# A state-space scan mixed with an FFT convolution on one core: the convolution rebuilt

## The chip, the cores and the metric

The kernel runs on one core of a Trainium2 chip. Its engines work beside each other, each through its own list of instructions in order: TensorE (PE) multiplies matrices into PSUM, with weight loads (PEld) as instructions of their own; VectorE (DVE) and ScalarE (ACT) compute on SBUF and PSUM; GpSimd (POOL) computes on SBUF and issues DMAs that add what they carry to what is there; SyncE (SP) issues plain and transposing DMAs. Sixteen DMA engines carry all transfers. Semaphores order the engines. The metric is the time of one execution on the device, in microseconds; lower is better.

## The reference

Two sequence models read the same x (2048 steps of 1024 channels, bf16) and a gate per step mixes them:

```python
g = sigmoid((x * gate_w).sum(-1, keepdims=True))
# a: a diagonal complex state space model with 1024 states
h = Lam_bar * h + Bu[:, t]            # for every t; Bu = x @ B_bar.T, complex
a = 2.0 * einsum(hseq, Cmat).real + x * Dskip
# b: a shift convolution of 4 taps, then a long one of 2048 taps, per channel
k_shift = sum over t of k_pad[:, t:t+S] * shift_k[:, ks-1-t]
kv = k_shift * v
y = irfft(rfft(pad(kv)) * rfft(pad(ssm_k)))[:S] + kv * ssm_D
b = x * y                             # q is x
out = g * a + (1 - g) * b             # g * a: also the term with Dskip
```

## The kernel before

**The long convolution (branch b)** is done by channels: 8 chunks `c` of 128 channels. A sequence of 2048 steps is cut into 4 blocks of 512. Each block is turned into 512 frequencies (four tiles `fi` of 128) by matmuls with tables of cosines and sines (CF, SF; NCF and NSF are negated halves), blocks are multiplied with one another, and a second pair of tables (CI, SI) brings the sums back. The tables use that a block can be split into an even and an odd part about its middle, which halves the matmuls: so every block is first folded, upper half plus and minus the mirrored lower half.

For chunk `c` the steps are:

- `load` (160): kT and vT, the channels of k and v with time along the row, and kn, the long kernel with time on the partitions, all by transposing DMAs of 512 KB.
- `taps` (430, through `tap_sums` 421): the 4 taps of the shift convolution as 16 matmuls of 512 columns, diagonal weights `dg` (built by `dgs` 252 on ACT), kT moving. ACT brings the sums to `ks`.
- `times_v` (454): DVE multiplies ks with vT, the lower halves of the blocks in reversed order (`lo`), the upper ones in place.
- `fold_V` (462): 16 matmuls of 256 columns turn the product to time on the partitions, and with the signs in PM at once into even and odd parts; 2 evacuations by ACT give `eov`.
- `fold_K` (406): the same for kn with an identity and a mirrored identity (`refl`) as weights: 8 matmuls of 512 columns, and two with one row that put ssm_D into the first tap; 2 evacuations give `eok`.
- `fwd_K` (475) and `fwd_V` (497): the spectra Kh and Vh, for half of the frequencies at a time (`hf`), so two tiles `fi` a call; an evacuation by ACT for each `fi`.
- `products` (511): for each half `hf` the complex products of all pairs of blocks whose sum of indices stays below 4: 8 products into scratch `t` and 11 sums into G, all on DVE.
- `inverse` (546): 32 matmuls of 512 columns from G, PSUM called psz, two evacuations to `cv`, and 4 DMAs that write the result to a scratch `cv_scr` in DRAM, laid out as [time, channel].

`turn_table` (373) makes one of 8 pairs of tables of turning angles for the scan (TC, TS, and TCi, TSi, scaled by the input gains); it is cut by `yield` into steps that are spread over the loop. `state_params` (312) does the small arithmetic of the states, on DVE.

**The state space model (branch a)** is done by blocks `tb` of 512 steps and groups `g` of 256 states. `Bu` (595) projects x: 32 matmuls of 512 columns and two evacuations to U. `scan` (606) on DVE turns U by the tables, runs 4 scans along time, and turns back, to `hb`. `Cy` (699) multiplies 128 steps of hb with CT (the transposed C) in 32 matmuls. `loads` (658) reads the rows of branch b from cv_scr (pbb) and of x; `scale_b` scales by 1 - g and adds the Dskip row with an adding DMA; `finish` (705) multiplies by x, adds both branches and stores.

**The order** is written out by hand. `put` (95) makes every instruction of an engine (DMA queues of SP and POOL too) follow the one issued before it, so the program's order is that of each engine. In the loop over chunks (764 to 819), for chunk `c` with n = c + 1 and nn = c + 2, PE does fold_K(n), half of the inverse of c - 1, half of fwd_K(n), fold_V(n), the other half of the inverse, half of fwd_V(n), taps(nn), and the other halves of fwd_K(n) and fwd_V(n), while DVE multiplies the spectra of chunk c. Buffers let PE run ahead: 6 half spectra (kvh), 4 half G, 4 + 3 scratch tiles (u4, w4), 3 double PSUM buffers and 2 single ones.

Lines 829 to 862 finish the convolution and interleave the last two turn tables with Bu of the first three groups. From 864 on come the tiles of the second part, the remaining Bu, and the loop (892) of one Cy, one Bu and one scan per turn; 8 of the 16 CT loads come before 862, 8 after it. From 911 on the last 512 steps: all groups but the last for 4 row tiles, then the last one in two halves.

Of the kernel before, what the change touches and what calls it, by code (L numbers as in the profile page):

```python
# [20 lines left out]
def kernel(  # L21
# [42 lines left out]
    NFI = 4  # L64

# [5 lines left out]
    cv_scr = dram.tile([S, D], BF16, name="cv_scr")  # L71
# [3 lines left out]
    wk = pool("wk", 3)  # L75
    wu = pool("wu", 4)
    psum = pool("psum", 3, space=bass.MemoryType.PSUM)
    psum1 = pool("psum1", 1, space=bass.MemoryType.PSUM)

    def w4(shape, dt, name):  # L80
        return wk.tile(shape, dt, name=name, tag="w4")
# [6 lines left out]

    def ps1(tag):
        return psum1.tile([128, 512], F32, name=tag, tag=tag)  # L90
# [25 lines left out]

    def copy(o, a):
        put("dve", V.tensor_copy, o, a)
# [21 lines left out]
    kv_pool = h3pool(h3, "kvh", 6)  # L140
    g_pool = h3pool(h3, "gh", 4)
    cv_pool = h3pool(h3, "cv", 2)
    tab_pool = h3pool(h3, "tab", 1)
    ld = h3pool(h3r, "ld", 3, side="right")
    ks_pool = h3pool(h3r, "ks", 2, side="right")
    eo_pool = h3pool(h3r, "eo", 2, side="right")
# [5 lines left out]
    prow = rows_[64:96, 0:128]  # L152

    nc.scalar.dma_start(out=skr, in_=B_shift_k.rearrange("(j p) k -> j p k", p=128))
    for i, ap in enumerate((A_Lambda_re, A_Lambda_im, A_log_dt, gate_w)):
        nc.scalar.dma_start(out=prow[i * 8:(i + 1) * 8, :], in_=ap.rearrange("(j p) -> j p", p=128))
# [4 lines left out]
    def load(which, c):  # L161
        cc = slice(c * 128, (c + 1) * 128)
        if which == "kn":

            t = ld.tile([128, NT, 128], BF16, name="kn", tag="ld")
            load_t(t, B_ssm_k[cc, :])
        else:
            t = ld.tile([128, S], BF16, name=which, tag="ld")
            load_t(t, (kf if which == "kT" else vf)[:, cc])
        lds[which, c] = t  # L170

    load("kT", 0)
    load("vT", 0)
# [5 lines left out]
    def load_BT(g):  # L179
        for c, src in enumerate((A_B_re, A_B_im)):  # L180
            load_t(BT[g][:, c], src[g * 256:(g + 1) * 256, :])

    def load_xT(tb, home=None):
        xT = (home or xt_pool).tile([128, ND, TB], BF16, name="xT")
        load_t(xT, xf[tb * TB:(tb + 1) * TB, :])
        xTs[tb] = xT
# [22 lines left out]
    def sincos(rq, n, sin_out, cos_out, sin_scale):  # L209

        fa = u4([128, n], F32, "fa")
        act(fa, rq, func=ACT.Abs)
        act(sin_out, rq, func=ACT.Sin, scale=sin_scale)
        act(cos_out, fa, func=ACT.Sin, bias=pih, scale=-TWO_PI)
# [7 lines left out]

    zeros = w4([128, 512], BF16, "zeros")
    put("dve", V.memset, zeros, 0.0)
    pih = consts.tile([128, 1], F32, name="pih")
    put("dve", V.memset, pih, math.pi / 2.0)
# [8 lines left out]
    colm_i = iota_i32([128, 2], [[256, 2]], 1, 2, "colm")  # L235
    fr_i = iota_i32([128, 2, 256], [[2, 2], [4, 256]], 1, 0, "fr_")
# [6 lines left out]
    pcol = consts.tile([128, 4 + KS, ND], F32, name="pcol")  # L243
    gwb = consts.tile([128, ND], BF16, name="gwb")
    psp = ps1("p1")[:, 0:32 + ND * KS]
    raise_clock(3)
    for k in range(KS):
        mm(psp[:, 32 + ND * k:32 + ND * (k + 1)], skr[:, :, k], ident[32:32 + ND, 32:32 + ND], True, True)
    raise_clock(6)
    copy(pcol[:, 4:], psp[:, 32:].rearrange("p (i j) -> p i j", j=ND))  # L250

    def dgs(c, on_dve=False):
        dg = ks_pool.tile([128, KS, 128], BF16, name="dg", bufs=1)
        for k in range(KS):
            if on_dve:
                ts(dg[:, k], ident, pcol[:, 4 + k, c:c + 1], None, ALU.mult)
            else:
                act(dg[:, k], ident, func=ACT.Identity, scale=pcol[:, 4 + k, c:c + 1])
        return dg

    dg0 = dgs(0, True)
    colm = consts.tile([128, 2], F32, name="colm")
    ts(colm, colm_i, 1.0 / 4096.0, None, ALU.mult)
    fr_ = u4([128, 512], F32, "fr_")
    copy(fr_, flat(fr_i))
    hf = u4([128, 2, 512], F32, "h")
    for mt in range(2):
        ts(hf[:, mt], fr_, colm[:, mt:mt + 1], None, ALU.mult)
    rqf = reduced(flat(hf), 1024)
    put("dve", V.scalar_tensor_tensor, out=flat(hf), in0=rqf, scalar=-1.0, in1=rqf, op0=ALU.mult, op1=ALU.max)  # L270
    PM = consts.tile([128, 2, 2, 128], BF16, name="PM")
    for a in range(2):
        for b in range(2):
            ts(PM[:, a, b], ident, -1.0 if a and b else 1.0, None, ALU.mult)

# [9 lines left out]
    def inverse_angles(h2):  # L285
        hi = (w4 if h2 else u4)([128, 2, 512], F32, "h")
        for k in range(2):
            fi = 2 * h2 + k
            ts(hi[:, k], trow[0], inv["col"][:, fi:fi + 1], inv["at0"][:, fi:fi + 1], ALU.mult, ALU.add)
        rq = (u4 if h2 else w4)([128, 1024], F32, "rq")  # L290
        ts(rq, flat(hi), MAGIC, -MAGIC, ALU.add, ALU.add)
        tt(flat(hi), flat(hi), rq, ALU.subtract)
        return flat(hi)

    def inverse_table(h2, rq):
        sincos(rq, 1024, flat(SI[:, 2 * h2:2 * h2 + 2]), flat(CI[:, 2 * h2:2 * h2 + 2]), -TWO_PI)


    Lre, Lim, logdt = pcol[:, 0], pcol[:, 1], pcol[:, 2]
# [4 lines left out]
    TC = rot_pool.tile([128, NP, TB], BF16, name="TC")  # L304
    TS = rot_pool.tile([128, NP, TB], BF16, name="TS")
    TCi = rot_pool.tile([128, NP, TB], BF16, name="TCi")
    TSi = rot_pool.tile([128, NP, TB], BF16, name="TSi")
# [4 lines left out]
    def state_params():  # L312

        mm(psp[:, 0:32], prow, ident[64:96, 64:96], True, True)
        copy(pcol[:, 0:4], psp[:, 0:32].rearrange("p (i j) -> p i j", j=ND))
        copy(gwb, psp[:, 24:32])
        yield
# [12 lines left out]
        for x, name in ((thn, "th"), (thU, "thU")):  # L330
# [4 lines left out]
            frs.append(fr)  # L335
        sc = []
# [11 lines left out]
        tt(rc, rv, cth, ALU.mult)  # L348
        rs = small("rs")
        tt(rs, rv, sth, ALU.mult)  # L350
        nre = small("nre")
        ts(nre, rc, -1.0, None, ALU.add)
        den = small("den")
        tt(den, Lre, Lre, ALU.mult)
        den2 = small("den2")
        tt(den2, Lim, Lim, ALU.mult)
        tt(den, den, den2, ALU.add)
        invden = small("invden")
        put("dve", V.reciprocal, invden, den)
        ts(invden, invden, 2.0, None, ALU.mult)  # L360
        t_a = small("t_a")
        t_b = small("t_b")
        tt(t_a, nre, Lre, ALU.mult)
        tt(t_b, rs, Lim, ALU.mult)
        tt(t_a, t_a, t_b, ALU.add)
        tt(c2r, t_a, invden, ALU.mult)
        tt(t_a, rs, Lre, ALU.mult)
        tt(t_b, nre, Lim, ALU.mult)
        tt(t_a, t_a, t_b, ALU.subtract)
        tt(c2i, t_a, invden, ALU.mult)  # L370
        ts(mc2i, c2i, -1.0, None, ALU.mult)

    def turn_table(pi, home):
# [4 lines left out]
        act(h, trow[0], func=ACT.Identity, scale=thn[:, pi:pi + 1])  # L378
        yield
        ts(rq, h, MAGIC, -MAGIC, ALU.add, ALU.add)  # L380
        tt(rq, h, rq, ALU.subtract)
        yield
        act(h, rq, func=ACT.Abs)
        act(TS[:, pi], rq, func=ACT.Sin, scale=TWO_PI)
        act(TC[:, pi], h, func=ACT.Sin, bias=pih, scale=-TWO_PI)
        yield
        m = home([128, 2, TB], BF16, "m")
# [3 lines left out]
        act(TCi[:, pi], TC[:, pi], func=ACT.Identity, scale=c2r[:, pi:pi + 1])  # L391
        act(TSi[:, pi], TS[:, pi], func=ACT.Identity, scale=c2r[:, pi:pi + 1])
        yield
        tt(TCi[:, pi], TCi[:, pi], m[:, 0], ALU.add)
        tt(TSi[:, pi], TSi[:, pi], m[:, 1], ALU.add)
# [4 lines left out]
    def rev(ap):  # L400

        return ap.rearrange("p (b t) -> p b t", t=512)[:, :, 255::-1]

    eos, kss = {}, {}

    def fold_K(c):
        kn = lds.pop(("kn", c))
        kb = kn.rearrange("p (a f) d -> p a f d", f=4)
        eo = eo_pool.tile([128, 2, 2, 4, 128], BF16, name="eok", tag="eo")
        for mt in range(2):  # L410
# [7 lines left out]
            act(eo[:, mt], ps, func=ACT.Copy)  # L418
        eos["k", c] = eo

    def tap_sums(ps, kT, dg, h):
        for b in range(2):
            t0 = (2 * h + b) * 512
            for i in range(KS):
                if t0 == 0:
                    mm(ps[:, b, i:512], dg[:, i], kT[:, 0:512 - i], i == 0, i == KS - 1)
                else:
                    mm(ps[:, b], dg[:, i], kT[:, t0 - i:t0 - i + 512], i == 0, i == KS - 1)

    def taps(c, dg):  # L430
        kT = lds.pop(("kT", c))
        ks = ks_pool.tile([128, S], BF16, name="ks")
        for h in range(2):
            ps = ps2([128, 2, 512], "taps")
            tap_sums(ps, kT, dg, h)
            act(ks[:, h * 1024:(h + 1) * 1024], flat(ps), func=ACT.Copy)
        kss[c] = ks

    def first_times_v(c, dg):

        kT, vT = lds.pop(("kT", c)), lds.pop(("vT", c))
        ks = ks_pool.tile([128, S], BF16, name="ks")
        lo = ks_pool.tile([128, 4, 256], BF16, name="lo", bufs=1)
        for h in range(2):
            ps = ps2([128, 2, 512], "taps")
            tap_sums(ps, kT, dg, h)
            hs = slice(h * 1024, (h + 1) * 1024)
            tt(lo[:, 2 * h:2 * h + 2], ps[:, :, 255::-1], rev(vT[:, hs]), ALU.mult)
            khi, vhi = (ap[:, hs].rearrange("p (b t) -> p b t", t=512)[:, :, 256:512] for ap in (ks, vT))
            tt(khi, ps[:, :, 256:512], vhi, ALU.mult)  # L450
# [512 lines left out]
```

## Time and profile before

| | us |
|---|---|
| median of 3 runs (442.76 to 444.92) | 444.85 |
| the profiled execution | 444.19 |
| its span, first to last instruction | 442.4 |
| PE busy | 423.1 |
| DVE busy | 421.9 |
| ACT busy | 260.3 |
| POOL busy | 27.1 |

The mean granted PE clock is 0.994. Busy times are sums over the whole span. The program has stages with different limits: the start (to about 56 us), the loop over chunks (to about 200), the end of the convolution (the last psz at 233.3), and the scan part to the end. Busy time in a stretch of one stage, and the chain of work that ended last, say what limits that stage. A row of a group of instructions gives the form, the count, the total busy time and the mean duration of one instruction, which for PE is longer than the distance between two, as matmuls overlap.

### The profile page before, as it was taken

Reading aid. Unit: us, or ns where it says so; the run is one execution under the profiler, and the core shown is the slowest. Engines: PE = TensorE matmul, PEld = TensorE weight load, DVE = VectorE, ACT = ScalarE, POOL = GpSimd, SP = SyncE. Lnnn points to the kernel's source line nnn. Section 1 sums busy time; section 2 is a strip of 40 time slices with the busy share of each in tenths; the row PEclk is TensorE's granted clock in tenths of the full one; section 3 lists DMA queues with packets and bytes.
Section 4 is the critical chain, followed back from the end, with each engine's and each line's share of the span. In section 5 each row is a group of like instructions: output and inputs, shape, how many; then the busy total and the mean of one; then the engine's idle time right before and its main releaser. Section 6 shows DMA issues by size and latency. Waiting matters only on the chain.

```text
span 442.4 us, 5684 instructions
## 1 busy us (share of the span) xinstructions
PE 423.1 (96%) x2104; PEld 199.4 (45%) x2142; DVE 421.9 (95%) x662; ACT 260.3 (59%) x320; POOL 27.1 (6%) x41
## 2 busy tenths in 40 slices
PE   8888899999999999979999999999999999999994
PEld 3434354544545454534444544444444444444442
DVE  7897999999999999999999999999999999999973
ACT  3796978979797979695552423443324432567102
POOL 2000000000000000000000000011011100223100
PEclk9998999999999999999999999999999999999999
DMA  7685294756558291135608941144474546297512
GB/s 144 144 134 105 49 184 100 140 111 149 125 102 184 60 205 24 25 68 100 115 12 159 176 135 24 25 119 111 99 172 96 147 139 166 38 207 162 118 45 98
DMA packets 128062, 49.94 MB, mean 113 GB/s; under 512 B 118169, under 2 KB 118177, under 8 KB 128034
## 3 DMA queue, kind: packets, MB, share of 16 engines
q1 hardware_dynamic: 123920, 42.22, 43.3%
q0 software_dynamic: 4032, 7.34, 9.6%
q8 instruction: 16, 0.26, 0.2%
q14 instruction: 12, 0.10, 0.1%
q10 hardware_dynamic: 82, 0.02, 0.0%
HBM read 8.67 MB, written 8.39 MB: 39 GB/s over the span
## 4 chain that ended last, share of the span: by engine, by line
PE 75%; DVE 12%; ACT 8%; issue 4%; DVEq 0%
PE bu L97 25%; PE psy L97 22%; PE psz L97 9%; PE psk L97 8%; DVE G L97 5%; DVE t L97 4%; PE taps L97 2%; PE foldk L97 2%; PE psv L97 2%; ACT Vh L97 2%; PE p L97 2%; PE foldv L97 2%; ACT eok L97 1%; ACT eov L97 1%; ACT Kh L97 1%
## 5 line engine op out<-in xcount | busy, mean ns | idle before, releaser
L97 PE MATMUL bu<-xT,BT 128*128 128x512 bf16 x499 | 111.6, 379 | 0.6
L97 DVE TENSOR_TENSOR t<-Kh,Vh 128x2048 bf16<-128x2048 bf16 (+3 forms) x128 | 102.3, 820 | 4.1 <-ACT SI L97 2.7
L97 PE MATMUL psy<-CT,hb 128*128 128x512 bf16 x470 | 105.2, 379 | 0.6
L97 PEld LDWEIGHTS <-BT 128*128 128x128 bf16 x512 | 50.0, 98 | 60.2
L97 PEld LDWEIGHTS <-hb 128*128 128x128 bf16 x512 | 49.9, 98 | 59.9
L97 DVE TENSOR_TENSOR G<-G,t 128x1536 bf16<-128x1536 bf16 (+2 forms) x144 | 69.4, 510 | 0.5
L97 ACT ACTIVATE U<-bu 128x1024 bf16<-128x1024 f32 x32 | 32.6, 1022 | 47.1 <-PE bu L97 42.3
L97 DVE TENSOR_TENSOR_SCAN W<-rv,init,A 128x512 bf16<-128x512 f32 x48 | 57.8, 1266 | 0.0
L97 PE MATMUL psz<-G,CI 128*128 128x512 bf16 x128 | 48.6, 379 | 2.0 <-DVE G L97 2.0
L97 PE MATMUL psz<-G,SI 128*128 128x512 bf16 x128 | 48.5, 379 | 0.0
L97 ACT ACTIVATE Kh<-psk 128x1024 bf16<-128x1024 f32 x32 | 32.6, 1028 | 10.7 <-PE psk L97 10.0
L97 ACT ACTIVATE ga<-psy,gcols 128x1024 bf16<-128x1024 f32 x8 | 8.9, 1114 | 46.3 <-PE psy L97 46.3
L97 PE MATMUL taps<-kT,dg 128*128 128x512 bf16 (+3 forms) x128 | 30.8, 385 | 1.6 <-ACT Vh L97 1.5
L97 ACT ACTIVATE Vh<-psv 128x1024 bf16<-128x1024 f32 x32 | 30.9, 1024 | 0.9 <-PE psv L97 0.9
L97 POOL DMA_DIRECT2D pbb<-gd x12 | 10.5, 871 | 342.4 <-ACT gd L97 330.3
L97 PE MATMUL psk<-eok,CF 128*128 128x512 bf16 (+1 forms) x96 | 26.5, 366 | 3.9 <-ACT eok L97 2.1
L97 ACT ACTIVATE cv<-psz 128x1024 bf16<-128x1024 f32 x16 | 16.4, 1027 | 23.0 <-PE psz L97 23.0
L97 PEld LDWEIGHTS <-CF 128*128 128x128 bf16 x160 | 15.7, 98 | 22.2 <-issue 7.0
L97 PE MATMUL psk<-eok,SF 128*128 128x512 bf16 (+1 forms) x89 | 24.7, 373 | 0.4
L97 ACT ACTIVATE BT<-psy,gcols 128x1024 bf16<-128x1024 f32 x6 | 6.7, 1111 | 30.6 <-PE psy L97 30.6
L97 PEld LDWEIGHTS <-SF 128*128 128x128 bf16 x160 | 15.9, 99 | 18.2 <-issue 3.5
L97 PE MATMUL psv<-eov,CF 128*128 128x512 bf16 x64 | 19.3, 379 | 3.0 <-ACT eov L97 2.2
(139 smaller groups left out, 570.0 us busy)
## 6 DMA issues: line engine op xcount, KB each, us to landing
cv_scr<-cv SPq DMA_DIRECT2D x32, 128.0 KB, 2.1
pbb<-cv_scr SPq DMA_DIRECT2D x12, 256.0 KB, 2.7
xr<-in_A_x_dram SPq DMA_DIRECT2D x12, 256.0 KB, 4.2
pbb<-gd POOLq DMA_DIRECT2D x12, 256.0 KB, 3.3
ga<-xr POOLq DMA_DIRECT2D x8, 256.0 KB, 3.3
out_dram<-ga SPq DMA_DIRECT2D x8, 256.0 KB, 2.0
out_dram<-BT SPq DMA_DIRECT2D x8, 256.0 KB, 2.0
BT<-cv_scr SPq DMA_DIRECT2D x4, 256.0 KB, 3.3
```

Of the source, the lines that this page charges most:

```text
L97: i = f(*a, **kw)
```

## The change

The convolution and the order of the loop are rewritten; the scan part keeps its instructions but for details.

- **v** is loaded as it lies, with time on the partitions, by plain DMAs: chunks 0 and 1 alone (256-byte rows), then two chunks in one DMA (512-byte rows).
- **Short taps**: kT becomes the weights and dg the moving operand, so the sums come out with time on the partitions: 64 matmuls of 128 columns a chunk, each with weights of its own, which start at PAD + t0 - i.
- **Mirroring**: fold_V and PM are gone. `mirror` turns the lower halves of the product with two matmuls; ACT copies them to `lo`; DVE subtracts for the even part, and an adding DMA makes the odd part in place. For the kernel `mirror_K` does so from chunk 3 on (two matmuls and one with one row, an extra copy by ACT); fold_K stays for chunks 0 to 2.
- **Products over all frequencies**: one call per chunk instead of two, with 8 products and 7 sums of twice the width, one of the sums (n1 into G) by an adding DMA. Chunk 0 is still done in halves; chunk 7 has no sum by DMA. Scratch lies in tiles that wait for B (BT[2], BT[3] holds every second Kh) and in WK.
- **Turn tables**: ACT does one more step (the rounding constant as a bias), DVE one instruction instead of four, the last sum is an adding DMA.
- `state_params` partly on POOL; the cv_scr layout is [chunk, 128, 4, 4, 128], so a store has 2 KB pieces and is one DMA per half, and `loads` reads 256-byte pieces.
- All 16 CT loads, and drow, now come after the last inverse; the scan's scratch w4 and hb lie where spectra and G did; PSUM is 4 double buffers; kvh holds 3 whole spectra, gh 2 whole G.
- The last Cy groups are no longer cut in halves, and the last row tile is stored in two halves.

```diff
-            t = ld.tile([128, S], BF16, name=which, tag="ld")
-            load_t(t, (kf if which == "kT" else vf)[:, cc])
+            move(t.rearrange("p n k d -> p n (k d)"),
+                 vf.rearrange("(n p) d -> p n d", p=128)[:, :, c * 128:(c + w) * 128])
...
+    def mirror_K(c):
+        kb = lds.pop(("kn", c)).rearrange("p (a f) d -> p f a d", f=4)
+        ps = ps2([128, 2, 4, 128], "mirror")
+        for mt in range(2):
+            mm(ps[:, mt], refl[:, 1], kb[:, 1 - mt], True, mt == 0)
+            if mt == 1:
+                mm(ps[:, mt, 0], refl[0:1, 1], sD[:, c * 128:(c + 1) * 128], False, True)
+        eo = eos["k", c] = eo_pool.tile([128, 2, 2, 4, 128], BF16, name="eok")
+        lo = eo_pool.tile([128, 2, 4, 128], BF16, name="lo", bufs=2)
+        act(lo, ps, func=ACT.Copy)
+        act(eo[:, 1], kb[:, 2:4], func=ACT.Copy)
+        yield
+        tt(eo[:, 0], kb[:, 2:4], lo, ALU.subtract)
+        gather(eo[:, 1], lo)
...
+    def tap_sums(kT, dg, h):
+        ps = ps2([128, 8, 128], "taps")
+        for n in range(8):
+            t0 = (8 * h + n) * 128
             for i in range(KS):
+                k0 = PAD + t0 - i
+                mm(ps[:, n], kT[:, k0:k0 + 128], dg[:, i], i == 0, i == KS - 1)
+        return ps
...
     def times_v(c):
+        ks, v = kss[c], lds.pop(("v", c))
+        tt(ks, ks, v.rearrange("p (b q) d -> p q b d", q=4), ALU.mult)
+        yield
+        lo = eo_pool.tile([128, 2, 4, 128], BF16, name="lo", bufs=2)
+        act(lo, mirror(c), func=ACT.Copy)
+        yield
+        e = eo_pool.tile([128, 2, 4, 128], BF16, name="ev")
+        tt(e, ks[:, 2:4], lo, ALU.subtract)
+        if c in (1, NC - 1):
+            tt(ks[:, 2:4], ks[:, 2:4], lo, ALU.add)
+        else:
+            gather(ks[:, 2:4], lo)
+        eos["v", c] = e, ks[:, 2:4]
...
+    def products(c, h=0, home=u4, by_dma=True):
...
+        mult(0, 0, None, G)
+        yield
+        n1 = mult(1, 0, W1)
+        if by_dma:
+            gather(G[:, :, 1:], n1)
+        yield
+        t2 = mult(0, 1, T2)
+        yield
+        n2 = mult(1, 1, W2)
+        if not by_dma:
+            tt(G[:, :, 1:], G[:, :, 1:], n1, ALU.add)
+        n3 = mult(2, 1, home([128, 4 * w], BF16, "t"))
+        tt(t2[:, :, 1:], t2[:, :, 1:], n2, ALU.add)
+        n2 = mult(3, 1, home([128, 2 * w], BF16, "t"))
+        tt(t2[:, :, 2:], t2[:, :, 2:], n3, ALU.add)
+        n1 = mult(2, 0, W2[:, 0:4 * w])
+        n3 = mult(3, 0, W2[:, 4 * w:])
+        tt(t2[:, :, 3:], t2[:, :, 3:], n2, ALU.add)
+        tt(n1[:, :, 1:], n1[:, :, 1:], n3, ALU.add)
+        yield
+        tt(G[:, :, 2:], G[:, :, 2:], n1, ALU.add)
+        yield
+        tt(G[:, 0], G[:, 0], t2[:, 1], ALU.subtract)
+        tt(G[:, 1], G[:, 1], t2[:, 0], ALU.add)
...
+    for c in range(NC - 1):          # chunk 0 has an order of its own
...
+        tabs, back, prod = turn_table(c - 1, u4), inverse(c - 1), products(c)
+        step(old)
+        step(tabs)
+        step(back)
+        step(tv)
+        steps(prod, 3)
+        run(tv)
+        step(old)
         if nn < NC:
             dg = dgs(nn)
+        run(back)
+        run(old)
+        if c in (1, 3):
+            load("v", c + 3)
+        fwd_K(n)
+        step(prod)
+        fk = none
         if nn < NC:
+            fk = mirror_K(nn)
+            step(fk)
+            taps(nn, dg)
+        step(tabs)
+        step(prod)
+        run(fk)
+        run(prod)
+        if nn < NC:
+            tv = times_v(nn)
+            step(tv)
+        fwd_V(n)
+        old = tabs
```

## The prediction

> **What bounds the kernel now.** I read the page's engine totals first, then busy time by stage, then the chain that ended last, then groups by shape, then the DMA queues.
>
> ```profile
> PE 423.1 (96%) x2104; PEld 199.4 (45%) x2142; DVE 421.9 (95%) x662; ACT 260.3 (59%) x320; POOL 27.1 (6%) x41
> ...
> q1 hardware_dynamic: 123920, 42.22, 43.3%
> q0 software_dynamic: 4032, 7.34, 9.6%
> ```
>
> Two engines are full, PE and DVE: a gain must relieve both. By stretch (columns: start:end and length, busy us of PE, PEld, DVE, ACT, POOL, PE clock, DMA share, GB/s):
>
> ```profile
> 97.41:121.66 24.25, 23.93 (x121) 11.76 (x122) 24.15 (x44) 20.92 (x29) 0.00 (x0) 1.00 0.61 130
> 170.00:195.00 25.00, 24.46 (x125) 12.14 (x126) 24.90 (x45) 20.62 (x26) 0.00 (x0) 1.00 0.17 32
> 226.00:248.00 22.00, 21.95 (x139) 10.54 (x139) 21.79 (x25) 6.98 (x7) 0.00 (x0) 1.00 0.66 123
> 340.00:380.00 40.00, 39.78 (x210) 18.59 (x214) 39.65 (x49) 14.82 (x16) 4.81 (x6) 1.00 0.51 134
> ```
>
> The convolution (until 233) has a period of 24.25 us per chunk of channels, later 25.0. From 226 on neither PE nor DVE idles, so everything after the last inverse transform is a fixed block: it ends at 233.3, PE is dense until 436.8, and 5.6 us follow, 209.1 in all. What is left is when that inverse ends. The chain through one chunk:
>
> ```profile
> 97.41 3.03 PE psk L97 x16
> 100.44 1.73 PE psv L97 x8
> 102.16 2.15 PE foldk L97 x10
> 104.31 3.56 PE psz L97 x16
> ...
> 110.89 1.75 PE foldv L97 x16
> ...
> 119.77 1.89 PE taps L97 x8
> ```
>
> This is PE's bill: psk 6.06, psv 3.46, foldk 2.15, psz 7.0, foldv 1.75, taps 3.46: 23.9 of 24.25.
>
> ```profile
> L97 DVE TENSOR_TENSOR t<-Kh,Vh 128x2048 bf16<-128x2048 bf16 x32 | 37.7, 1219 | 1.2 <-ACT Kh L97 1.2
> L97 DVE TENSOR_TENSOR t<-Kh,Vh 128x512 bf16<-128x512 bf16 x32 | 13.5, 421 | 0.0
> L97 PE MATMUL foldv<-PM,ks 128*128 128x256 bf16 x64 | 14.5, 273 | 0.0
> L97 PE MATMUL p<-gwb,xT 128*128 128x1 bf16 x128 | 3.6, 163 | 0.0
> ```
>
> The DVE rows give (1219-421)/1536 = 0.52 ns an element; starts in the timeline (0.60 us for 1024, 0.87 for 1536) add 0.067 us an instruction. By that, products cost 22.1 us a chunk, times_v 1.2, the turn table 1.7: 25.0, the later period.
>
> **The change part by part, per chunk in the steady loop.**
>
> *PE.* foldv goes (-1.75); mirror of v is 2 matmuls of 512 at 0.216 (+0.43). foldk becomes 2 matmuls and a one-row one, 0.65 (-1.5, chunks 3 to 7 only). The taps turn from 16 matmuls of 512 columns into 64 of 128, each with weights of its own. foldv starts a weight load and 256 columns every 0.109 us (512 columns take 0.216), so its loads are hidden; the gate's pairs with one column come every 0.78/32 = 0.024. Half of 0.109 is 0.055, 3.5 us a chunk as before; unhidden it is 0.055+0.024 = 0.079, 5.1 us; the far end, a price of 0.109, is 7.0. I take 0.055, as all the loads of foldv, the nearest row, were hidden. Sum 3.46+0.43+3.46+6.06+0.65+3.5+3.46 = 21.1 (22.7 unhidden).
> The Trainium skill (TensorE: Matmul & The Clock Gate, Back-to-back issue gap) speaks against this: it gives about 81 ns for a weight load and matmul of 128 columns; by that the sum below would end near 428, as the first rival does. Its 131 ns for 512 columns disagrees with the 216 seen here, so this rule gets the smaller chance.
>
> *DVE.* Products over all frequencies are 15 instructions instead of 38: products 2x2.2+2x1.67+2x1.13+2x0.60 = 11.2; sums 1.67+4x1.13+2x0.60 = 7.4; 18.6 together. One sum of 3072 elements (1.67) has gone to DMA. times_v 1.13, the even part of v 0.60, of the kernel 0.60, the turn table one instruction 0.6. Sum 21.5 against 25.0.
>
> *ACT.* 14 evacuations of 0.92, a copy 1.04, dg 1.15, turn table 5.2: 20.3 against 20.9. It was covered by 24.25; now it is the third engine within a microsecond of the period. Followed in program order, each evacuation still ends before PE wants its PSUM buffer back (four of two banks, were three and two single ones), so I charge nothing; the cover is those four buffers.
>
> *The loop.* The first product of a chunk needs its last Vh, and the next inverse needs the last G. Two periods hold at least one DVE pass from first product to last G (20.4), one PE pass (21.1), two evacuations at the turn (1.3) and semaphores (0.2): 43.0, so 21.5 a period. All three engines and the loop give 21.5: no cover is left.
>
> *Sums by DMA, all on POOL's queue in one order:* n1 into G 786 KB, v's and the kernel's mirrors 262 each, a turn table 262: 1.57 MB. q0 took 9.6% of 442.4 = 42.5 us for 7.34 MB, 173 GB/s: 9.1 us of all engines. Transposes: kT, kn and one of BT or xT, 1.57 MB; the stretch at 97.41 moved 24.25x130 = 3.15 MB in 0.61x24.25 = 14.8 us, 213 GB/s (188 in the stretch before): 7.9. v by plain DMA 0.52 on average, cv 0.52 in 2 KB pieces: 4.5. Total 21.5 of 21.5; before 15. DMA goes from 0.65 to nearly full. What waits: G[2:] is 12.4 us behind the issue of n1's sum; fwd_V of the odd part some 11 behind the mirror's sum, which queues behind n1's. A 256 KB sum landed after 3.3 us (median; 6.2 at most), so three times that is 10 to 19. Bounds of the cost: 0 to 7 us a period. I take 0.8 for this and all small waits, near the low end, as 10 fits: T = 22.3.
> By the Trainium skill (DMA: Bandwidth & Descriptors, Issuing engines are not separate DMA queues) POOL's sums and SP's transposes interleave on the same 16 engines, so neither queue is a way around the other; no trace of before has both dense at once.
>
> *SP's order:* kn, kT, one 512 KB load, the two cv stores (were four), v every second chunk. A late cv holds back what is behind it, as today; kn and kT are issued some 4 us before the period and wanted 13 into it.
>
> *Start.* DVE's first product was at 21.7, chunk 1 began at 50.2 with ACT full (11.0 of 11 from 44). After: DVE work ahead of the first product sums to about 21; state arithmetic on POOL frees 2.5 us of DVE, but the reciprocal now waits for POOL with the products behind it (0 to 3). ACT has about as many instructions until the second chunk's spectrum. I take DVE's chunk 1 at 50.5 and PE's first inverse at 49.5 (was 55.7, as foldv and foldk were longer; 45 if ACT does not hold it, 55 if nothing is saved).
>
> *End of the convolution.* Chunk 6 on PE has no taps and kernel: 16.9. Then Bu of three groups and two inverses, 5x6.9 = 34.5, while the last products (20.3) and two tables (1.2) run on DVE. The loads of BT[2] and [3] wait until chunk 6's products leave these tiles, then have 20 us for 4x3. Last inverse: 49.5+5x22.3+16.9+34.5 = 212.4.
>
> *After it.* All 16 CT loads now follow the last inverse (8 before). At 1.34 us an issue: 2.1 for cv, 5.2 for xT, 21.4, landing 4: 33, and the first Cy wants them at 36. Zero, with 0 to 5 as bounds. pbb arrives in 256-byte rows, four times the time of 2.7 us at most, still under the 14 us lead: zero. Scan tiles lie where spectra did, free when the last products end. The tail: DVE ended 2.2 us behind PE, now a half-row pair 1.4: -0.7.
>
> *Sum.* 212.4+209.1-0.7 = 420.8 of span. Profiled execution: 444.19 for 442.4 of span, so +1.8; the median of the runs, 444.85, lies 0.66 above that execution: 423.2.
>
> **The rivals.**
> *Taps not hidden* (0.079): PE 22.7, T 23.0 with small waits, start +1: 50.5+115+16.9+34.5 = 216.9, 427.8 in all. For it: no row has 128 columns, and tap offsets give odd weight addresses. Against: foldv.
> *DMA is the bound:* v comes in pairs, so chunks 1 and 3 need up to 25, and at 188 GB/s more; T 25 gives 49.5+125+51.4 = 225.9, 436.7. For it: 21.5 of 21.5. Against: BT, xT and v are wanted only later, so a lag is absorbed at first, and the last chunks load less.
> *Slower: n1's sum lands too late.* DVE is in order; G[2:] blocks G's closing pair, v's product and thus inverse and spectrum. Equal to before means T = (233.3+0.7-49.5-51.4)/5 = 26.6, that is 5.1 us over 21.5, a landing 17.5 us after issue. At 19 us T is 28.1, the inverse ends at 241.4: 452. For it: 6.2x3 = 18.6. Against: the median, 10, and traffic that comes in bursts.
>
> **How the numbers follow.** Forecast 0.55; taps 0.15; DMA bound 0.15; late sum 0.12; something else, both sides, 0.03. Likeliest: 423, with its own range 418 (T 21.5, start 48) to 428 (T 23.1 and a start 0.5 later). The range of 8 in 10 goes from 415 (T 21.5, start 45) to 440, which takes in the taps and the DMA bound up to a T of 25.7, and leaves out the late sum and some of the something else. Within 0.5% (2.2 us, about what a measurement here can tell from nothing) only a T of 26.1 to 27: 0.03. Faster 0.84, slower 0.13.
>
> **What would show it.** foldv gone; taps 512 of 128 columns, their 64 in 3.5 us (5.1 if unhidden); product rows of 4096 elements at 2.2 us; PE's period between two mirror groups 22.3; n1's landing under 12 us; DMA share near 0.9 in 50 to 180; last psz at 212 and 208 from there to the end. Wrong if G waits for DMA, if PE waits for ACT's Vh or ks by more than 1 us a chunk, or if the scans wait for CT.

## The result, and the profile after

The changed kernel takes 429.28 us in the median of four executions (422.72 to 437.60), beside 443.89 us for the kernel before on the same chip: a ratio of 0.958, 95% interval 0.947 to 0.969. The forecast was 423 (415 to 440). The ratio is taken from the two shorter executions (the medians as they stand give 0.967), and the profiled one, 430.88 us with a span of 429.1, is one of the two longer ones. A repetition (below) gave 424.78 us (422.32 to 428.75), ratio 0.956 (0.952 to 0.961).

The page's totals and the two large DMA queues, after:

```profile
PE 405.1 (94%) x2340; PEld 202.4 (47%) x2378; DVE 398.9 (93%) x459; ACT 254.1 (59%) x310; POOL 69.2 (16%) x90
...
q1 hardware_dynamic: 117648, 42.22, 46.6%
q0 software_dynamic: 8528, 17.17, 24.5%
```

PE has lost 18.0 us of work and DVE 23.0, while the span is only 13.3 us shorter. So both stand idle for longer than before: PE for 24.0 us instead of 19.3, DVE for 30.2 instead of 20.5. POOL rose from 27.1 to 69.2 us. Busy time by stretch shows where the idle time lies (columns as in the prediction):

```profile
66.00:70.00 4.00, 0.00 (x0) 0.00 (x0) 0.00 (x0) 0.00 (x0) 0.00 (x0) 0.96 1.30 70
70.00:74.00 4.00, 0.00 (x0) 0.00 (x0) 0.00 (x0) 0.00 (x0) 0.00 (x0) 0.50 0.77 103
...
108.55:130.12 21.57, 21.16 (x148) 11.77 (x149) 21.57 (x20) 20.40 (x28) 3.92 (x5) 1.00 0.97 172
130.12:151.69 21.57, 21.16 (x148) 11.80 (x149) 21.57 (x21) 20.43 (x28) 3.92 (x5) 1.00 1.19 183
```

The steady loop is what the change promised: a period of 21.57 us, DVE busy for all of it. But from 66 to 74 nothing computes at all, and from 66 to 70 the DMA engines, at a busy share of 1.30, move 70 GB/s. (The share adds up the times of packets, which can overlap, so it can pass 1.) The chain that ended last goes straight through it:

```profile
39.68 3.38 POOL rc L91
...
47.47 2.14 POOL c2r L91
...
51.27 2.22 POOL t_b L91
...
55.85 1.08 POOL mc2i L91
56.93 0.05 POOL kT L91
56.98 0.79 POOL G L91
57.77 19.94 DMA ks<-lo
77.75 5.95 PE psv L91 x14
```

Small state arithmetic holds POOL's queue until 56.9; behind it wait the sums of chunk 1, n1 (in the tile `wkh`) into G and v's mirror `lo` into `ks`. The first takes 19.5 us from issue to landing, the second 19.94, and DVE and PE wait for them:

```profile
PE psv L91 <- DMA ks<-lo: 13.5, 1, 13.5
DVE G L91 <- DMA G<-wkh: 12.8, 1, 12.8
```

Each of the two happens once ("1" is the number of times). The 14 matmuls behind the wait took 5.95 us instead of 14x0.216 = 3.0, for the granted clock had gone to 0.50 while PE stood. Chunk 1 lasts 37.4 us on PE (its first psz at 46.15, the next chunk's at 83.52), 15.8 more than a period. What SP and POOL issued at that time (start, length of the issue):

```profile
55.13 0.44 SPq L91 DMA_DIRECT2D v<-in_B_v_dram  x1
55.67 6.64 SPq L91 DMA_TRANSPOSE kn<-in_B_ssm_k_dram  x1
```

```profile
56.93 1.24 POOL L91 DMA_DIRECT2D G<-wkh  x1
57.77 1.33 POOL L91 DMA_DIRECT2D ks<-lo  x1
```

So the sums go to the DMA engines just behind 1 MB of v and the transposes of kn. The data of n1 was ready at 51.1, that of `lo` at about 54: by these times both sums would have been ahead of v without POOL's small work. Chunk 3 of the same profile shows that case: v's other load and transposes come there too, at 114.58 and 115.85, but the sums leave ahead of them, at 110.61 and 113.42, and nothing waits.

### The profile page after: what moved, and what is told of

Its sections match the earlier page's. It is cut to its first block, busy times and chain, and to the rows that moved or that the text cites. A ratio compares the mean times of both kernels' runs of the same rounds, so it can differ in the third digit from the quotient of the medians.

```text
span 429.1 us, 6062 instructions
## 1 busy us (share of the span) xinstructions
PE 405.1 (94%) x2340; PEld 202.4 (47%) x2378; DVE 398.9 (93%) x459; ACT 254.1 (59%) x310; POOL 69.2 (16%) x90
## 4 chain that ended last, share of the span: by engine, by line
PE 67%; DVE 18%; DMA 5%; POOL 4%; issue 4%; ACT 1%; DVEq 0%; ACTq 0%; POOLq 0%
PE psy L91 26%; PE bu L91 26%; DVE wkh L91 5%; DVE BT L91 5%; PE psz L91 5%; DMA ks<-lo 5%; PE psk L91 4%; DVE G L91 3%; PE psv L91 3%; PE taps L91 2%; DVE t L91 2%; DVE ks L91 1%; PE foldk L91 1%; POOL t_a L91 1%; PE p L91 1%
## 5 line engine op out<-in xcount | busy, mean ns | idle before, releaser
L91 PE MATMUL psy<-CT,hb 128*128 128x512 bf16 x502 | 111.4, 379 | 0.6
L91 PE MATMUL psv<-ks,SF 128*128 128x512 bf16 x64 | 20.6, 407 | 13.8 <-DMA ks<-lo 13.5
L91 PE MATMUL taps<-dg,kT 128*128 128x128 bf16 x512 | 31.4, 223 | 0.0
L91 PEld LDWEIGHTS <-kT 128*128 128x128 bf16 x512 | 30.0, 100 | 0.8 <-issue 0.2
L91 DVE TENSOR_TENSOR G<-G,wkh 128x2048 bf16<-128x2048 bf16 (+3 forms) x11 | 12.6, 1147 | 12.8 <-DMA G<-wkh 12.8
L91 PE MATMUL psk<-eok,CF 128*128 128x512 bf16 (+1 forms) x89 | 24.0, 360 | 0.0
L91 ACT ACTIVATE BT<-psy,gcols 128x1024 bf16<-128x1024 f32 x5 | 5.6, 1114 | 30.3 <-PE psy L91 30.3
L91 DVE TENSOR_TENSOR wkh<-BT,Vh 128x3072 bf16<-128x3072 bf16 (+4 forms) x20 | 21.9, 1116 | 0.0
L91 DVE TENSOR_TENSOR wkh<-Kh,Vh 128x3072 bf16<-128x3072 bf16 (+2 forms) x16 | 21.4, 1356 | 0.0
```

The lines of the kernel that those rows point to most:

```text
L91: i = f(*a, **kw)
```

## The experiments

The profile left two sides to blame: POOL's, whose small work sends the sums off late, and that of the DMA engines, which get v's load and the transposes just then. A third reading was formed after the first four runs: neither alone, but the order in which v, the transposes and the sums reach the engines. The last three runs ask which of these partners are needed (theories A and B there). Each run goes with the expectation written before it. All ratios are to the kernel before, on the same chip.

**State arithmetic back on DVE.**

```diff
-        put("pool", nc.gpsimd.tensor_tensor, out=o, in0=a, in1=b, op=op)
+        put("dve", V.tensor_tensor, out=o, in0=a, in1=b, op=op)
...
-        put("pool", nc.gpsimd.tensor_scalar, out=o, in0=a, scalar1=s1, scalar2=None, op0=op)
+        put("dve", V.tensor_scalar, out=o, in0=a, scalar1=s1, scalar2=None, op0=op)
```

> The state arithmetic goes back from POOL to DVE; all else as in the changed kernel. Theory 1 (POOL late): in the changed kernel the small instructions hold POOL from 39.7 to 56.9, so chunk 1's n1 sum is issued 5.8 us and the mirror's sum 3.5 us after its data is there, and both land after 19.5 to 20 us instead of the 7.3 of the later chunks. Then here n1 is issued by 52, both land by 63, PE's wait for the mirror's sum (13.5) falls below 1 us, and the span is 429.1 - 15.8 (chunk 1 took 37.4 instead of 21.6) + 2.5 (DVE) = 416, 418 in all, with little spread. Theory 2 (burst): the 1 MB of v, kn and cv issued from 50.9 to 55.7 fill the DMA engines whatever POOL does; then a wait of 8 us or more stays and the time is 424 or more.

Measured: 416.50 us (416.33 to 416.81), ratio 0.939 (0.936 to 0.942). POOL's issues, and how long the sums into G took to land, in two views:

```profile
53.22 1.21 POOL L91 DMA_DIRECT2D G<-wkh  x1 [15.35 <-DVE wkh L91]
56.01 0.89 POOL L91 DMA_DIRECT2D ks<-lo  x1 [1.59 <-DVE ev L91]
...
DMA to landing us min/median/max: 6.6/6.8/7.7
```

SP issued v at 55.84 and kn at 57.24. So n1's sum is now ahead of v, the mirror's 0.17 us behind it, and both are ahead of the transposes; none into G or ks takes over 7.7 us. PE has no wait for `ks` left, and the spread of the times went from 15 us to 0.5. So in the changed kernel the stall needs this arithmetic on POOL, and v's load, which comes at about the same time as there, is not enough for it. Whether POOL's work does it, or only the order that follows from it, this run doesn't say.

**v later, state arithmetic still on POOL.** v's load for chunks 4 and 5 goes behind the transposes of kn and kT at the start of the next turn of the loop.

```diff
+        if c == 2:
+            load("v", 4)
...
-        if c in (1, 3):
+        if c == 3:
             load("v", c + 3)
```

> The 1 MB of v for chunks 4 and 5 is loaded a chunk later, ahead of that chunk's 512 KB load; the state arithmetic stays on POOL. Theory 1 (POOL late): both sums are still issued at about 57 and 58, and the wait of PE for the mirror's sum stays above 8 us, 426 or more. Theory 2 (burst): with a third of the traffic gone the sums land after 7 to 9 us, at 65 to 66; the wait is 1 to 3 us, 418 to 420.

Measured: 416.17 us (415.80 to 416.39), ratio 0.938 (0.935 to 0.942). The sums leave as late as before, at 56.99 and 57.82, behind kn (55.19), but v now follows at 67.91. They land within 8.9 us, and PE waits 1.0 us:

```profile
PE psv L91 <- DMA ks<-lo: 1.0, 1, 1.0
```

POOL is as busy as in the changed kernel, the sums are as late, and the stall is gone: POOL's side alone is not enough either.

**Twice the state arithmetic on POOL.** The last nine small operations are done a second time, into scratch that nobody reads.

```diff
+        ptt(u_a, nre, Lre, ALU.mult)
+        ptt(u_b, rs, Lim, ALU.mult)
...
+        pts(u_c, u_c, -1.0, ALU.mult)
```

> The last nine small instructions of the state arithmetic are done twice on POOL, the second time into scratch that nobody reads; all else as in the changed kernel. Theory 1 (POOL late): some 10 us more on POOL, the sums issued at 67 or later, PE's wait 13.5 + 5 to 10, and the time 434 to 442. Theory 2 (burst): the sums land when the burst is over, at about 77 as now, and the time stays within 3 us of the changed kernel's.

Measured: 424.32 us (423.08 to 425.63), ratio 0.957 (0.952 to 0.961). The sums leave at 64.58 and 65.42, when v (issued at 55.22) has landed after 6.2 us, and take 6.6 and 7.1. The waits:

```profile
DVE G L91 <- DMA G<-wkh: 7.3, 1, 7.3
```

The sums leave 7.6 us later than in the changed kernel, and DVE waits 7.3 for them: with v out of the way, lateness costs about what it is late. PE waits 2.6 for `ks`, and 3.8 for another thing that the doubled work holds back on POOL, the zeros that POOL writes into the padding of kT for the taps. The time is that of the changed kernel (ratio 0.957 beside 0.958 and, in the repetition below, 0.956): more of the suspected cause did not make the kernel slower, since it moved the sums out of v's way. Beside the repetition the number is what the side of the DMA engines gives, but by that side the sums should land at about 77, and they land at 71.2 and 72.5.

**The sums on DVE again** (n1, and both mirrors).

```diff
-        gather(eo[:, 1], lo)
+        tt(eo[:, 1], eo[:, 1], lo, ALU.add)
...
-            gather(ks[:, 2:4], lo)
+            tt(ks[:, 2:4], ks[:, 2:4], lo, ALU.add)
...
-        tabs, back, prod = turn_table(c - 1, u4), inverse(c - 1), products(c)
+        tabs, back, prod = turn_table(c - 1, u4), inverse(c - 1), products(c, 0, u4, False)
```

> The three sums of the convolution's loop (n1 into G, both mirrors) are made by DVE instead of by DMA; the turn tables' sums stay DMAs, the state arithmetic stays on POOL. DVE gets 1.67 + 2 x 0.60 = 2.87 us a chunk more, so if DVE sets the period it goes from 21.6 to 24.4, and no sum can be late: 413.3 (the span without chunk 1's stall) + 5 x 2.87 + 1.7 = 429.4, 431 in all. Rival: DMA at 0.9 to 1.2 of its engines is what holds the period, and then it stays below 23 and the time below 423.

Measured: 431.72 us (431.02 to 432.03), ratio 0.973 (0.970 to 0.976). The page:

```profile
PE 405.9 (95%) x2340; PEld 201.5 (47%) x2378; DVE 414.9 (97%) x475; ACT 254.3 (59%) x310; POOL 52.8 (12%) x74
```

DVE has 16 us more than the changed kernel (16 instructions: 1.75 for n1 and twice 0.69 for mirrors a chunk), PE the same, and in the loop neither waits for a DMA. Two periods in a row are 26.0 and 23.1 us, 24.6 in the mean, so the rival of a period below 23 is out. Against the versions without a stall on the same chip (416.2 to 416.5) the sums by DMA are worth 15 us, more than half of the 26.6 that the change can bring there (before: 442.91); the rest of it is worth 11.

**The changed kernel again**, unedited, to see how the stall varies.

> The changed kernel again. The four times so far are 422.7 to 437.6, while the variants without the stall stay within 0.6 us. If the stall of chunk 1 is where two streams of DMAs meet, its length differs from execution to execution and everything else does not: period 21.6, PE's wait for the mirror's sum between 4 and 20 us, the time 413.3 + 1.8 + that wait and up to 3 us of slow PE clock behind it.

Measured: 424.78 us (422.32 to 428.75). Its profiled execution has a span of 420.5, 8.6 less than the first. Its wait, and its DMA from 66 to 70:

```profile
PE psv L91 <- DMA ks<-lo: 5.1, 1, 5.1
```

```profile
66.00:70.00 4.00, 0.22 (x1) 0.10 (x1) 0.82 (x1) 0.00 (x0) 0.00 (x0) 0.65 0.99 183
```

The wait is 8.4 us shorter than in the first profile, which is nearly the whole difference of the spans. The issues lie in the same order (v 55.60, kn 56.13, sums 57.40 and 58.23); the sums land after 11.7 and 11.5 us, at 183 GB/s, not 70. By these two executions the stall has two parts: standing behind v and kn, which costs some 5 us of waiting in both (1.0 of them is lateness alone, by the run with v later), and a slow stretch on top, which came in one of them.

**Late sums without state arithmetic on POOL.** State arithmetic on DVE as in the first experiment, but POOL copies 2x1024 elements to a scratch nobody reads before it issues chunk 1's sum.

```diff
+        if c == 1:
+            late = m_pool.tile([128, 2, TB], BF16, name="m")
+            for i in range(2):
+                put("pool", nc.gpsimd.tensor_copy, flat(late), W1[:, i * 2 * TB:(i + 1) * 2 * TB])
```

> State arithmetic on DVE as in the first experiment, but before chunk 1's n1 sum POOL copies 2 x 1024 elements of the product, so that both sums are issued some 4 us later, behind the 1 MB of v, with no state arithmetic on POOL. Theory 3 (order: a sum issued while v and kn are in flight ahead of it crawls; one issued before v does not): landing of 12 us or more, PE waits 6 or more, 424 to 436. Theory 4 (lateness alone: a sum issued 4 us late lands 4 us late, as with the doubled state arithmetic): landing 7 to 8, PE waits 0 to 3, 417 to 420.

Measured: 430.12 us (426.96 to 432.40), ratio 0.970 (0.965 to 0.975).

```profile
PE psv L91 <- DMA ks<-lo: 15.4, 1, 15.4
```

```profile
66.00:70.00 4.00, 0.00 (x0) 0.00 (x0) 0.55 (x1) 0.00 (x0) 0.00 (x0) 0.90 1.23 82
```

The stall is back, slow stretch included, with the sums at 56.80 and 57.54 behind v (55.24) and kn (55.78), landing after 21.4 and 22.2 us. So it takes late sums, whatever on POOL makes them late.

**The same with v later.** The edits of the second and of the last experiment together.

> As the run before it, with the 1 MB of v moved a chunk later as in the second experiment. Theory 3 (order): no v ahead of the sums, landing 7 to 9, PE waits 0 to 3, 417 to 420, so below the run before it by 6 or more. Theory 4 (lateness alone): the same time as the run before it, within 2 us.

Measured: 418.07 us (417.94 to 418.72), ratio 0.943 (0.942 to 0.945): sums late (57.77, 58.51), v at 68.59, landing within 7.6 us, no stall.

**State arithmetic on DVE and v later.**

> State arithmetic on DVE and v a chunk later together. Either alone removed the stall (416.5 and 416.2), so together they add nothing: 2.5 us more for DVE at the start against 1 us less of waiting, 415.5 to 417, with a spread under 1 us. If a wait were still hidden in either, it would be below 415.

Measured: 416.23 us (416.10 to 417.02, five executions), ratio 0.9395 (0.938 to 0.941). Either edit alone gives all there is to gain; none of the three stands out as the best.

**Which of the three partners?** Two runs with the sums late by POOL's copies. First kn behind kT:

```diff
-            load("kn", nn)
+            if c != 2:
+                load("kn", nn)
             load("kT", nn)
+            if c == 2:
+                load("kn", nn)
```

> Chunk 1's sums late by the POOL copies as before, v's load still ahead of them, but the transposes of kn are issued only behind kT's, some 8 us later. Theory A (the slow stretch needs v's 1 MB load ahead and the sums behind it, the transposes don't matter): the sums of n1 and of v's mirror land 15 to 22 us after issue, the time is 426 to 433. Theory B (it is the transposes of kn, run together with the sums and behind v, that make it slow): both sums land within 9 us, and kn comes some 8 us late, which its own taker has in reserve in part: 416 to 422.

Measured: 430.58 us (428.19 to 431.55), ratio 0.969 (0.964 to 0.973); sums landing after 20.5 and 21.3 us, PE's wait 14.5. The number is theory A's, but the run doesn't decide, for kT found a free buffer and took kn's place:

```profile
55.29 0.44 SPq L91 DMA_DIRECT2D v<-in_B_v_dram  x1
55.82 5.84 SPq L91 DMA_TRANSPOSE kT<-in_B_k_dram  x1
```

It shows only that it needn't be kn. In the second, the transposes go first and v right behind them:

```diff
             load("kn", nn)
+            if c == 2:
+                load("v", 4)
             load("kT", nn)
...
-        if c in (1, 3):
+        if c == 3:
             load("v", c + 3)
```

> Sums late by the POOL copies, the transposes of kn first, then v's load right behind them, at about the sums' own issue. Theory A: v is no longer ahead, the sums land within 9 us or so: 416 to 420. Theory B: transposes and sums are in flight together, with v beside them: landings of 15 to 22 us again and 425 to 433. A third outcome, landings of 10 to 14 us and 418 to 424, would say that all three share the DMA engines and that it is a matter of bytes in flight alone.

Measured: 419.61 us (419.22 to 419.74), ratio 0.946 (0.943 to 0.948): kn at 56.22, sums at 57.77 and 58.51, v at 58.41. All three are in flight together, the bytes are the same, and the sums land after at most 8.9 us; the four times lie within 0.5 us. Theory B as written (transposes and sums together are enough) falls: for this stall v has to be issued earlier. Whether it has to be ahead of the transposes or ahead of the sums this run doesn't separate, for it moves v behind the transposes and behind the first sum.

**No transposes behind v.** Sums late, v ahead, but kn, kT and BT issued only behind the next chunk's stores.

```diff
-            load("kn", nn)
-            load("kT", nn)
+            if c != 2:
+                load("kn", nn)
+                load("kT", nn)
...
         run(back)
         run(old)
+        if c == 2:
+            load("kn", nn)
+            load("kT", nn)
+            load_BT(1, 0)
```

> Chunk 1's sums late by the POOL copies and v's load ahead of them as before, but the transposes of kn, kT and BT are issued only behind the next chunk's stores, some 18 us later: between v's load and these stores no transpose is in flight. Theory A (v's load ahead of the sums is enough): the two sums land 15 to 22 us after issue, and PE waits for ks by 10 us or more. Theory B (v's load, a transpose behind it, and the sums behind both): the sums land within 9 us, PE's wait for ks is under 3 us. In both the late kn and kT cost something, estimated at 0 to 10 us over 418 by B, over 430 by A.

Measured: 430.16 us (426.63 to 435.90), ratio 0.967 (0.962 to 0.972). Here the time says little and the trace much. With v at 55.64 and no transpose until 80.10, the sums, issued at 57.20 and 57.93, land after 8.7 and 9.2 us; the loads and sums of the stretch from 54 to 70 (KB, us to landing):

```profile
v<-in_B_v_dram SPq DMA_DIRECT2D x1, 1024.0 KB, 6.7
G<-wkh POOLq DMA_DIRECT2D x1, 768.0 KB, 8.7
```

So v alone does not do it, as far as one execution of a stretch that varies can tell. The time is lost later, by the edit itself: PE waits 7.5 us for kn, and in the profiled execution a slow stretch comes at 140 to 148 (76 GB/s), with kn's transposes of a later chunk in flight (an issue of 13.76 us) and a wait of 5.4 for `ks`, this time with no load of v running. So a slow stretch can come without v.

Taken together, for chunk 1: sums issued behind v and a transpose landed after 11.5 to 22.2 us (the changed kernel twice, and the two late versions with 430.12 and 430.58 us); with any one of the three moved (sums ahead of the transposes, v behind them, no transposes, or v landed already) they landed within 9.2. The DMA view shows the standing behind: from 58 to 64 POOL's queue moved 0.04 MB in the first profile and 0.15 in the repetition, while SP's moved 1.18 and 1.32; with v behind the transposes it moved 0.69, without transposes 0.63. It also shows what slow means: from 64 to 70 of the first profile SP's queue has 245 packets (0.06 MB) with 52.0% of the time of the 16 engines, which is 0.20 us a packet; from 70 to 76 of the repetition 3321 packets (0.84 MB) take 66.1%, 0.02 us each.

What starts a slow stretch, and why it doesn't come in each execution, is open. In each one looked at a transpose was in flight, but transposes are in flight for much of the steady loop too, at 172 to 183 GB/s, so this shows a companion and not a cause. No run varied the size of v's pieces or of the transposes.

## Why the prediction was right, and where not

The sum can be gone through against the profiled execution (span 429.1, predicted 420.8). The last inverse ends at 221.4, where 212.4 was forecast:

| step | predicted | measured | adds to the span |
|---|---|---|---|
| PE's first inverse of chunk 1 | 49.5 | 46.15 | -3.35 |
| period T, five times | 22.3 | 21.57 in four | -3.65 (five at 21.57) |
| chunk 6 and to the last inverse | 51.4 | 51.6 | +0.2 |
| after it, with the tail | 208.4 | 207.7 | -0.7 |
| stall in chunk 1 | none | 37.4 instead of 21.57 | +15.8 |

420.8 - 3.35 - 3.65 + 0.2 - 0.7 + 15.8 = 429.1. The kernel without the stall thus comes to 413.3 of span, and the stall-free versions measured 414.0 to 414.8: the table holds. The median of 429.28 lies in the range of 415 to 440, and 1.3 above the likeliest's own 418 to 428. That the span is off by 8.3 us and not by 15.8 is luck: the stall, for which the sum has no term, took 15.8, and the start and the period came out 7.0 shorter than forecast.

**PE's bill** was right: 21.1 predicted (its terms as written add up to 21.0), 21.16 measured. The taps were the open term. The timeline has the 64 of a chunk as one entry:

```profile
119.21 3.75 PE L91 MATMUL taps<-dg,kT 128*128 128x128 bf16 x64
```

One matmul lasts 0.22 from start to end, so the starts are (3.75-0.22)/63 = 0.056 apart, the 0.055 taken from foldv: the loads are hidden, and that rival is out. The Trainium skill (TensorE: Matmul & The Clock Gate, Back-to-back issue gap) gives about 81 ns for such pairs; the trace does not agree, it has 56.

**DVE's bill** was right: 21.5 against 21.57, and DVE never stops in the steady loop. A product of 4096 elements costs what the slope said: two starts in chunk 1, at 47.25 and 49.46, are 2.21 apart, and the group's mean of 2289 ns runs from the start to the end of one:

```profile
L91 DVE TENSOR_TENSOR G<-Kh,Vh 128x4096 bf16<-128x4096 bf16 x4 | 9.2, 2289 | 0.0
```

ACT's 20.3 was 20.40. **The small waits** of 0.8 a period were not there: all four steady periods are DVE's own sum.

**The sums by DMA** in the steady loop were oversized: a landing of 10 to 19 after issue was expected by three times the 256 KB row, and the median was 7.5 for 768 KB (6.6 to 7.7 in the run without the stall). The share of the DMA engines in the four steady periods was 0.72 to 1.19, about what was feared, and the period did not care. The rival "DMA is the bound" is out for this loop: a share of 1 is not the end of what these engines can take.

**The start** came 3.35 us earlier than taken, inside its bounds of 45 to 55. The reciprocal's wait for POOL was 1.1 of the 0 to 3. Which term of the start was too long no run shows.

**The step that failed** is "state arithmetic on POOL frees 2.5 us of DVE, but the reciprocal now waits for POOL with the products behind it (0 to 3)". It asked who waits for a result of this work, and not what is queued behind it on POOL, where the prediction itself had put all the sums "in one order". It gave this work no duration on POOL. Before, DVE did the same 16 operations and the reciprocal among them in 2.6 us, from the first of these lines to the second:

```profile
33.97 0.16 DVE L97 TENSOR_TENSOR rc<-rv,th_cos 128x8 f32<-128x8 f32 x1
36.38 0.17 DVE L97 TENSOR_SCALAR mc2i<-c2i 128x8 f32<-128x8 f32 x1
```

On POOL they took from 39.7 to 56.9, 17.2 us, and held n1's sum back by 5.8 us and with it the mirror's, past v's load and kn. The prediction's own sign, "Wrong if G waits for DMA", came true in this one chunk (12.8 us). The third rival had the right wait, "n1's sum lands too late", and nearly the right landing (19.5 us, where 17.5 would decide), but as a matter of every chunk with a full queue. It came once, because of what was issued ahead of it in chunk 1; so it cost 15.8 us, and not the 29 by which that rival lay above the forecast.

**After the last inverse** all was as charged: neither PE nor DVE has a wait for CT from 221.4 on, the landing of CT being 4.2 us.

## What to carry to other kernels

When work moves to an engine that also issues DMAs, charge its whole duration there to everything queued behind it, above all DMAs that somebody waits for, and ask what other queues will have issued in the meantime. Two full engines that stand idle together in one short stretch are worth a look before the steady loop is tuned further: here either of two edits of a few lines took another 8 to 13 us off (424.8 or 429.3, to 416.2 or 416.5). A time that varies by several per cent between executions can be one wait of varying length; the difference of two profiles' waits (8.4 us here) against the difference of their spans (8.6) shows it.

## What the hardware did that was not expected

- Operations on 128x8 elements cost 0.16 to 0.17 us on DVE before, and 0.19 to 3.38 on POOL. They were short (0.19 to 0.24 each) from 43.0 to 44.1, where DVE stood idle, and longer (0.53 to 3.38) beside DVE's products and sums:

```profile
43.04 0.19 POOL L91 TENSOR_TENSOR rs<-rv,th_sin 128x8 f32<-128x8 f32 x1
...
51.23 2.25 POOL L91 TENSOR_TENSOR t_b<-nre,pcol 128x8 f32<-128x8 f32 x1
```

  The Trainium skill (GPSIMD Engine Reference, Specifications) says that GpSimd's SBUF interfaces are shared with VectorE, with contention where a DVE instruction has two inputs in SBUF. The trace agrees in that the long ones, up to 3.38 us, all lie beside such instructions; no run here varied DVE's inputs alone.
- The DMA engines can be busy by their share (1.30 of 16 engines' time) and move 70 GB/s, less than half of the 172 to 183 of the steady loop.
- PE's granted clock fell to 0.50 some time after its last matmul: 5.5 us after it in the first profile (work until 64.2; a mean of 0.85 from 69 to 70, 0.50 from 70), 2.6 in the repetition (64.7; 0.61 from 67 to 68). It stayed there for the first matmuls after the wait: 2.9 us on top of 13.5 in the first profile.
